# x of tiles 6 to 15 transposed by SBUF-to-SBUF transfers and 32x32 transposes on VectorE, and the low parts of the k and v weights on VectorE

## The chip, the cores and the metric

The kernel runs on one core of one Trainium2 chip. The metric is the device time of one execution in microseconds (us). Before the change its median is 504.29 us over three runs (504.22 to 504.36). Beside these runs one execution was profiled; the rows quoted below are from it, and their times count from the start of its span.

## The reference

x has 2048 positions of 512 features. It is normalised, put through an attention with 32 heads of 16 features, in which each position looks at 8 positions at a distance of 2 (itself, 2 back, ... 14 back), and the result is gated by the silu of a two-layer network on the same normalised x.

```python
def _A_ref(x, wqkv, wo):
    B, S, D = x.shape
    H = 32; Dh = D // H
    W, dil = 8, 2
    qkv = (lambda x, *d: x.transpose(*d))((x @ wqkv).reshape(B, S, 3, H, Dh), 2, 0, 3, 1, 4)
    q, k, v = qkv[0], qkv[1], qkv[2]
    ...
    logits = jnp.einsum("bhsd,bhswd->bhsw", q, kg) * scale
    logits = jnp.where(mask[None, None, :, :], logits, -1e9)
    attn = _softmax(logits, axis=-1)
    o = jnp.einsum("bhsw,bhswd->bhsd", attn, vg)
    return (lambda x, *d: x.transpose(*d))(o, 0, 2, 1, 3).reshape(B, S, D) @ wo

def _B_ref(x, w1, b1, w2, b2):
    h = jnp.einsum("bsd,df->bsf", x, w1) + b1
    zero = jnp.zeros_like(h)
    r = jnp.where(h > zero, h, zero)
    h = r * r
    out = jnp.einsum("bsf,fd->bsd", h, w2) + b2
    return out

x = A_x
xn = _layernorm(x, axis=-1)
s = _A_ref(xn, A_wqkv, A_wo)
g = _silu(_B_ref(xn, B_w1, B_b1, B_w2, B_b2))
return x + s * g
```

## The kernel before

**Numbers in two parts.** Every product is made of three passes (`PASSES`): each operand is split in a high part, which ScalarE copies to the matmul's type (`high`), and a low part, which is the difference (`low`, a subtraction on VectorE or on POOL). High times high, high times low and low times high are added up in PSUM. So a product of a tile with a 512-wide weight is 12 matmuls: four pieces of the inner dimension by three passes.

**Stage 1: tiles of x.** x goes through in 16 tiles of 128 positions, worked in pairs. For a tile `t`, `mean`, `spread` and `norm` compute the normalised rows `xn` on ScalarE and POOL. `trans` turns them with four 128x128 transposes on TensorE into a PSUM tile `pxT` (two buffers), ScalarE copies the high part of the result, and `lowx` makes the low part on VectorE. Then `qkv(t, s)` multiplies by the three parts of wqkv (s = 0, 1, 2 for q, k, v), `evacuate` copies the product to `stg`, and a transfer per pair and part takes it to DRAM (`sq`, `sk`, `sv`). From tile 4 on the transposed tile also goes to DRAM (`sx`), for stage 2.

**Stage 2: the network, in four chunks of four tiles.** For each of 14 slices f of the hidden layer, `up(c, f)` makes the hidden values `ph` (12 matmuls); ScalarE applies relu and squares it twice, once for the high part `h`, once in place; `lowh(f)` makes the low part on VectorE. `down(pb, f, j)` adds its product with w2 to `pb` (12 matmuls for the four tiles). `down` follows `up` two slices behind. `ph` has two PSUM buffers (`psH`), so `up(c, f + 2)` cannot start before `lowh(f)` has read `ph` of slice f. At the end of a chunk `gate` applies the bias `b2t` and silu to `pb`, giving `z`.

**Attention, on VectorE.** It is done in eight units u of 256 positions. q, k, v of a unit are loaded from DRAM. `qk(u, s)` is a multiplication over 128x2048 into `pr` and a reduction of it (a pair), four pairs a unit; `soft_a` and `soft_b` are the softmax around an exponential on ScalarE; `av(u, s)` is a multiplication into `pv` and a reduction into `v`, again four pairs a unit. The stream runs qk of unit u, then av of unit u - 1, the last unit's av at the end. `store(u)` writes the result to DRAM (`so`), `load_o(u)` reads it back in four transfers (`oq`), `trans_o` turns it in 32x32 blocks on VectorE, and `lowo` makes its low part. `out_product` multiplies by wo (`pw`), and `finish` multiplies with `z`, adds x and writes the output.

**The order.** All engines take their instructions in an order that the program fixes. For the attention the program keeps two planned clocks, `clock["PE"]` and `clock["V"]`, which add a price per instruction (227 ns a matmul, 150 ns a transpose, elements over 0.96 plus 170 ns on VectorE). `pump(margin)` puts the next steps of the attention stream into VectorE's queue as long as VectorE's planned clock stays under TensorE's plus the margin. `load_o(u)` needs `store(u)`, and puts whatever is left before it into the queue at once:

```python
    def load_o(u):
        while done_units[0] <= u:
            flush(None)
            pump(clock["V"] - clock["PE"] + 4000)
```

In chunk c, `load_o(2c)` stands at f = 7, ahead of `lowh(7)`, and `load_o(2c + 1)` at f = 12, ahead of `lowh(12)`; `trans_o` of the first two tiles stands at f = 10. For the last chunk, units 6 and 7 are thus stored, read back and transposed within the chunk.

Transfers from SP's queue go in SP's order; loads of q, k, v and of the transposed x (`xU`) go from ScalarE's queue. In the profile all instructions of the helper `Ordered` carry line 76, so rows are told apart by tile names.

Of the kernel before, what the change touches and what calls it, by code (L numbers as in the profile page):

```python
# [8 lines left out]
F32 = mybir.dt.float32  # L9
FR = mybir.dt.float32r  # L10
AF = mybir.ActivationFunctionType
# [25 lines left out]

WARM = 18
WARM2 = 3

MATMUL, TRANSPOSE, DVE_FIXED, SLACK, LATE, ROOM = 227, 150, 170, 500, 3000, 1000

# [4 lines left out]
def body(ctx: ExitStack, tc: tile.TileContext, x, wqkv, wo, w1, b1, w2, b2, out):  # L47
# [119 lines left out]
    mhalf = const.tile([P, 1], F32, name="mhalf")  # L167
    G.memset(mhalf, -0.5)
    mask = const.tile([P, BI, W], F32, name="mask")
    zero = px.tile([HALO, 4, P], F32, name="zero")  # L170

    def constants():
        G.memset(zero, 0.0)
        for t in (sk, sv):
            dma(t[:, :HALO, :].rearrange("g h c -> h g c"), zero)
        G.memset(mask, 0.0)
        for blk in (1, 0):
            for w in range(W):
                n = max(0, min(BI, (W - 1 - w) * DIL - blk * BI))
                if n:  # L180
                    G.memset(mask[:4 * blk + 4, :n, w], -1e9)

    b1t = const.tile([P, NF], F32, name="b1t")
    b2t = const.tile([P, D], F32, name="b2t")

    sq = dram.tile([4, S, P], F32, name="sq")
    sk = dram.tile([4, HALO + S, P], F32, name="sk")
# [187 lines left out]


    NT = S // P
    mv, means, rs, shifts, xn, pTs, xt, xT, seen = {}, {}, {}, {}, {}, {}, {}, {}, {}

    def moments(t, st):  # L380
        mv[t] = px.tile([P, 2], F32, name=f"mv{t}", tag="mv", bufs=2)
# [21 lines left out]
        G.tensor_mul(shifts[t], means.pop(t), rs[t])  # L403

    def norm(t):
        xn[t] = px.tile([P, D], F32, name=f"xn{t}", tag="xn", bufs=2)
        if t < 2:
            n = D // 2 if t == 0 else D
            for i in range(0, D, n):
                V.tensor_scalar(xn[t][:, i:i + n], xins[t][:, i:i + n], mv[t][:, 0:1], rs[t],  # L410
                                op0=OP.subtract, op1=OP.mult)
            del xins[t]
        else:
            A.activation(xn[t], xins.pop(t), AF.Identity, bias=shifts.pop(t), scale=rs[t])
        if t + 4 < NT:
            load_x(t + 4)

    def place(t):
        if t < TPC:
            xt[t] = xT[0][:, t]  # L420
        else:
            xt[t] = pxT.tile([P, 2, KT, P], FR, name=f"xt{t}", tag="xt", bufs=4)

    def trans(t):
        place(t)
        pTs[t] = psT(f"pxT{t}")
        for kt in range(KT):
            PE.transpose(pTs[t][:, kt * P:(kt + 1) * P], xn[t][:, kt * P:(kt + 1) * P], ident)
        seen[t] = clock["PE"] + 800
        A.activation(xt[t][:, 0], pTs[t].rearrange("p (k n) -> p k n", k=KT), AF.Copy)  # L430

    def lowx(t):
# [60 lines left out]

    def lows(s, kt):
        low(*wq_parts(s, kt), V)
        low(*wq_parts(s, kt + 1), G)


    sts = [px.tile([P, 6], F32, name=f"st{t}", tag="st", bufs=2) for t in range(2)]
# [17 lines left out]
    norm(1)  # L517
    for kt in range(1, KT):
        split(*wq_parts(0, kt), V)
    split(xt[0][:, 0], xt[0][:, 1], x0.rearrange("p (k n) -> p k n", k=KT), V)  # L520
    ps = psA("pq0_0")
    for kt in range(KT):
        if kt == KT - 1:
            trans(1)
        PE.matmul(ps, x0[:, kt * P:(kt + 1) * P], raws[0, kt], start=kt == 0, stop=kt == KT - 1)
    lowx(1)
    evacuate(0, 0, ps)
    highs(1, 0)
    lows(1, 0)
# [28 lines left out]
    for a in range(2, NT, 2):  # L558
        b, more = a + 1, a + 2 < NT
        later = a + 4 < NT  # L560

        def weights(f):
            if 0 <= f < NKEEP:
                load_w(keep, f)
            if 0 <= f - 1 < NKEEP:
                split_w(f - 1)

        if later:
            mean(a + 4)
        qkv(a, 0)  # L570
        if more:
            trans(a + 2)
        pump(LATE)
        qkv(b, 0)
        weights(a - 5)
        if more:
            lowx(a + 2)
            trans(b + 2)
        if later:
            mean(b + 4)  # L580
        pump(LATE)
        qkv(a, 1)
        if later:
            spread(a + 4)
        if more:
            lowx(b + 2)
        pump(LATE)
        if not more:
            up(0, 0)
        qkv(b, 1)  # L590
        if later:
            spread(b + 4)
        if not more:
            pump()
            up(0, 1)
            lowh(0)
        weights(b - 5)
        pump(LATE)
        qkv(a, 2)
        if later:  # L600
            norm(a + 4)
        pump(LATE)
        qkv(b, 2)
        if later:
            norm(b + 4)
        if a == NT - 4:
            dma(b1t, b1.rearrange("(f p) -> p f", p=P))
            dma(b2t, b2[None, :].to_broadcast([P, D]))
        if a >= TPC:
            for t in (a, b):  # L610
                dma(sx[t // TPC][:, t % TPC], xt.pop(t).bitcast(F32))
        pump(LATE if more else -SLACK)
# [66 lines left out]
        dma(tile_rows(out, t)[:, cols], z[:, cols])  # L679

    wot = p2.tile([P, 2, 4, 512], FR, name="wot")

    for c in range(NCH):
        last = c == NCH - 1
        pb = [psA(f"pb{c}_{j}") for j in range(TPC)]
        t0 = c * TPC
        for f in range(2, NF):
            if c == 0:
                for i in (6, 7) if f == 2 else (f + 5,):
                    if i < NF:  # L690
                        load_w(p2, i)
            up(c, f)
            pump()
            if c == 0 and f == 3:

                rwo = [p2.tile([P, 2, D], F32, name=f"rwo{i}", tag="oT", bufs=2) for i in range(2)]
                for i in range(2):
                    for q in range(4):
                        rows = wo[q * P + 64 * i:q * P + 64 * i + 64, :].rearrange("(g p) n -> p g n", g=2)
                        dma(rwo[i][32 * q:32 * q + 32], rows)  # L700
            if c == 0:
                if NKEEP <= f + 3 < NF:
                    split_w(f + 3)
                if 6 <= f < 10:
                    split(wot[:, 0, f - 6], wot[:, 1, f - 6], rwo[(f - 6) // 2][:, (f - 6) % 2], G)
            elif f == 2:
                finish(t0 - 4, G)
                finish(t0 - 3, G)
            elif f == 3:
                load_r(t0 - 2)  # L710
                load_r(t0 - 1)
                trans_o(t0 - 2, psT(f"pT{t0 - 2}"))
                trans_o(t0 - 1, psT(f"pT{t0 - 1}"))
            elif f == 4:
                lowo(t0 - 2)
                lowo(t0 - 1)
            elif f == 5:
                out_product(t0 - 2, psT(f"pw{t0 - 2}"))
            elif f == 6:
                finish(t0 - 2, G)  # L720
                out_product(t0 - 1, psT(f"pw{t0 - 1}"))
            elif f == 7:
                finish(t0 - 1, G)
            if f == 7:
                load_o(c * 2)
            if f in (9, 10) and not last:
                load_r(t0 + f - 9)
            if f == 10:
                for i in range(2):
                    trans_o(t0 + i, psT(f"pT{t0 + i}"))  # L730
            if f == 11:
                for i in range(2):
                    lowo(t0 + i)
            if f == 12:
                load_o(c * 2 + 1)
            if not (last and f == NF - 1):
                for j in range(TPC):
                    down(pb, f - 2, j)
            pump(ROOM if c else -SLACK)
            lowh(f)  # L740
        for j in range(2):
            out_product(t0 + j, psT(f"pw{t0 + j}"))
        pump()
        if not last:
            for i in range(2):
                for j in range(TPC):
                    down(pb, NF - 2 + i, j)
                pump()
            for i in range(2):
                up(c + 1, i)  # L750
            for j in range(TPC):
                gate(c, j, pb)
            lowh(0)
            lowh(1)
            pump()
        else:
            for i in range(2, TPC):
                trans_o(t0 + i, psH(f"pT{t0 + i}"))
            for i in range(2, TPC):
                lowo(t0 + i)  # L760
            xl = xTa.tile([P, TPC, 512], F32, name="xlast", tag="xT")
            dma(xl.rearrange("p (h e) n -> p h (e n)", e=2),
                x[t0 * P:(t0 + TPC) * P, :].rearrange("(h p e) n -> p h (e n)", p=P, e=2))
            for j in range(TPC):
                for f in range(NF - 3, NF):
                    down(pb, f, j)
                gate(c, j, pb)
                if j < 2:
                    finish(t0 + j, V, xl[:, j])
            for j in range(2, TPC):  # L770
                n = D // 2 if j == TPC - 1 else D
                for i in range(0, D, n):
                    cols = slice(i, i + n)
                    out_product(t0 + j, (psT if i else psH)(f"pw{t0 + j}_{i}"), cols)
                    finish(t0 + j, V, xl[:, j], cols)


# [19 lines left out]
```

## Time and profile before

| | us |
|---|---|
| median of three runs | 504.29 |
| the profiled execution's own time | 504.34 |
| its span | 502.3 |
| TensorE (PE) busy | 494.2 (98%) |
| VectorE (DVE) busy | 418.1 (83%) |
| ScalarE (ACT) busy | 218.8 (44%) |
| POOL busy | 107.8 (21%) |

The page has an execution in rows by engine. PE is the matmuls, PEld the loading of weights beside them, SPq and ACTq the instructions that issue transfers. A row of the timeline has start and duration in us, engine, line, operation, tile written and tiles read, shapes, how many instructions were merged, and in brackets how long the engine had been idle before and what ended that. In a row of a group the two numbers after the first bar are the busy time in us and the mean duration of one in ns, and after the second bar stands the idle time before. The chain of waits follows the end of the execution back to what released each step.

Stage 1 runs to about 160 us (the products of the last pair are mixed with the first `up`), and the chunks begin at about 141, 231, 318 and 405 us.

### The profile page before, as it was taken

The numbers are of one execution on the slowest core, as the hardware profiler recorded it, in microseconds if no ns is written. First come the engines' busy times: TensorE is split into PE (matmuls) and PEld (weight loads), VectorE is DVE, ScalarE is ACT, GpSimd is POOL, SyncE is SP. The second block draws the span as 40 slices with busy tenths as digits, with TensorE's granted clock in tenths as the row PEclk, the third lists the DMA queues.
The fourth block names the chain that finished last, engine by engine and source line by source line (L and its number), as shares of the span: only waits on it lengthen the run. The fifth ranks groups of instructions, "written<-read, shape, count | busy, mean of one in ns | idle before, by whom it ended". The sixth has DMA issues, their size and how long they took to land.

```text
span 502.3 us, 5930 instructions
## 1 busy us (share of the span) xinstructions
PE 494.2 (98%) x2202; PEld 405.9 (81%) x2202; DVE 418.1 (83%) x334; ACT 218.8 (44%) x397; POOL 107.8 (21%) x125
## 2 busy tenths in 40 slices
PE   8899999999999999999999999999999999999996
PEld 5688888888888888888888888888888888888885
DVE  5217999987999999995799999399899949998926
ACT  5855456663242555513632341362253146414322
POOL 1622345861000588300203000021200002120000
PEclk9999999999999999999999999999999999999999
DMA  8979489689664757261433406125230822311052
GB/s 293 278 245 393 179 260 317 230 277 372 231 240 134 253 146 241 84 242 43 127 157 100 172 11 267 58 85 201 82 148 11 299 67 85 136 64 42 4 164 84
DMA packets 45064, 85.64 MB, mean 171 GB/s; under 512 B 4988, under 2 KB 28908, under 8 KB 42220
## 3 DMA queue, kind: packets, MB, share of 16 engines
q1 hardware_dynamic: 40716, 51.72, 31.2%
q10 hardware_dynamic: 4320, 33.56, 18.1%
q8 instruction: 17, 0.28, 0.2%
q14 instruction: 11, 0.09, 0.1%
HBM read 57.94 MB, written 27.32 MB: 170 GB/s over the span
## 4 chain that ended last, share of the span: by engine, by line
PE 95%; DVE 1%; DMA 1%; POOL 0%; issue 0%; SPq 0%; ACT 0%; DVEq 0%
PE ph L76 30%; PE pb L76 30%; PE pq L76 25%; PE pw L76 8%; PE pxT L76 1%; DMA wqraw<-in_A_wqkv 1%; DVE z L76 1%; DVE wq L76 0%; SPq L144 0%; POOL wq L76 0%; DVE xT L76 0%; SPq L134 0%; POOL rs L76 0%; ACT z L76 0%; ACT stg L76 0%
## 5 line engine op out<-in xcount | busy, mean ns | idle before, releaser
L76 PE MATMUL pb<-w,h 128*128 128x512 f32 x672 | 160.6, 389 | 0.0
L76 PEld LDWEIGHTS pb<-w,h 128*128 128x128 f32 x672 | 126.2, 188 | 26.2
L76 ACT ACTIVATE ph<-ph,b1t 128x512 f32<-128x512 f32 x56 | 37.0, 661 | 196.4 <-PE ph L76 191.9
L76 PE MATMUL ph<-xU,w 128*128 128x512 f32 x504 | 120.7, 390 | 0.0
L76 PEld LDWEIGHTS ph<-xU,w 128*128 128x128 f32 x504 | 94.4, 188 | 20.4 <-DVE h L76 0.9
L76 PE MATMUL pq<-wq,xt 128*128 128x512 f32 x432 | 101.3, 392 | 0.0
L76 PEld LDWEIGHTS pq<-wq,xt 128*128 128x128 f32 x432 | 80.3, 188 | 16.5
L76 DVE TENSOR_TENSOR pr<-k,q 128x2048 f32<-128x2048 f32 x32 | 75.6, 2362 | 10.4 <-DMA k<-sk 10.0
L76 DVE TENSOR_TENSOR pv<-v,L 128x2048 f32<-128x2048 f32 x32 | 75.9, 2373 | 0.4
L76 DVE TENSOR_REDUCE L<-pr 128x128 f32<-128x2048 f32 x32 | 73.1, 2284 | 0.7
L76 DVE TENSOR_REDUCE v<-pv 128x256 f32<-128x2048 f32 x32 | 72.9, 2278 | 0.6
L76 POOL TENSOR_TENSOR z<-z,xr 128x512 f32<-128x512 f32 x12 | 21.2, 1778 | 220.4 <-DVE z L76 215.7
L76 DVE TENSOR_TENSOR h<-ph,h 128x512 fp32r<-128x512 f32 x56 | 38.4, 686 | 31.2 <-ACT ph L76 30.9
L76 ACT ACTIVATE stg<-pq 128x512 f32<-128x512 f32 x48 | 28.6, 596 | 57.8 <-PE pq L76 52.6
L76 PE MATMUL pw<-wot,oT 128*128 128x512 f32 (+1 forms) x204 | 45.5, 376 | 0.0
L76 PEld LDWEIGHTS pw<-wot,oT 128*128 128x128 f32 x204 | 36.8, 188 | 7.1
L76 PE MATMUL ph<-xT,w 128*128 128x512 f32 x168 | 40.5, 390 | 0.0
L76 POOL TENSOR_TENSOR w<-w1r,w 128x512 fp32r<-128x512 f32 x14 | 24.3, 1735 | 68.8 <-ACT w L76 66.2
L76 PEld LDWEIGHTS ph<-xT,w 128*128 128x128 f32 x168 | 31.5, 188 | 6.7
L76 PE MATMUL pq<-wq,xT 128*128 128x512 f32 x132 | 32.9, 402 | 1.8 <-POOL wq L76 1.5
L76 ACT ACTIVATE h<-ph 128x512 fp32r<-128x512 f32 x56 | 33.5, 599 | 1.8
L76 ACT ACTIVATE ph<-ph 128x512 f32<-128x512 f32 x56 | 33.3, 595 | 0.0
(64 smaller groups left out, 318.9 us busy)
## 6 DMA issues: line engine op xcount, KB each, us to landing
k<-sk ACTq DMA_DIRECT2D x8, 1408.0 KB, 8.6
v<-sv ACTq DMA_DIRECT2D x8, 1408.0 KB, 9.4
sx<-xt SPq DMA_DIRECT2D x12, 512.0 KB, 7.6
xU<-sx ACTq DMA_DIRECT2D x6, 1024.0 KB, 8.2
x<-in_A_x SPq DMA_DIRECT2D x16, 256.0 KB, 4.2
sq<-stg SPq DMA_DIRECT2D x8, 512.0 KB, 4.1
sk<-stg SPq DMA_DIRECT2D x8, 512.0 KB, 6.9
sv<-stg SPq DMA_DIRECT2D x8, 512.0 KB, 3.2
```

Source lines behind the costliest of these rows:

```text
L76: return tc.keep_in_program_order(f(*a, **k))
```

## The change

**Tiles 6 to 15 (`TURN` = 6).** `norm` writes a pair of tiles into one buffer, in which the 512 features are grouped in four blocks a, each with the 32 features a of every 128. `shuffle` then moves the pair with four SBUF-to-SBUF transfers of 128 KB each, issued from SP: block a of position 4p + b goes to partition 32a + p, place b. `trans` turns the moved tile `xb` with a single VectorE instruction of 32x32 transposes, whose output in PSUM steps by 4 elements, so that the positions come out in their order. The four TensorE transposes of these tiles are gone; ScalarE's copy and `lowx` stay. `mean`, `spread` and `norm` of the pair after next stand earlier in the loop, and `trans` and `lowx` of the next pair one product later.

**The k and v weights' low parts.** `lows` computes every second one on VectorE in place of POOL, four in all. At the start `lowx(1)` stands ahead of the low part of tile 0.

**Other moves.** `zero` lies in a buffer of the attention's, `b2t` in stage 2's memory and is loaded at its start. The last product of tile 15 is split in 256, 128 and 128 columns, where it was 256 and 256.

```diff
     def lows(s, kt):
         low(*wq_parts(s, kt), V)
-        low(*wq_parts(s, kt + 1), G)
+        low(*wq_parts(s, kt + 1), V)
...
     def norm(t):
-        xn[t] = px.tile([P, D], F32, name=f"xn{t}", tag="xn", bufs=2)
+
+        if t < TURN:
+            xn[t] = px.tile([P, 2, D], F32, name=f"xn{t}", tag="xn", bufs=2)[:, 0]
+        elif t % 2 == 0:
+            xn[t] = px.tile([P, 4, 2, P], F32, name=f"xn{t}", tag="xn", bufs=2)
...
         else:
-            A.activation(xn[t], xins.pop(t), AF.Identity, bias=shifts.pop(t), scale=rs[t])
+
+            A.activation(xn[t // 2 * 2][:, :, t % 2].rearrange("p a (k c) -> p k a c", k=KT),
+                         xins.pop(t).rearrange("p (k a c) -> p k a c", a=4, k=KT),
+                         AF.Identity, bias=shifts.pop(t), scale=rs[t])
...
+    def shuffle(t):
+
+        src = xn.pop(t)
+        xb[t] = px.tile([P, 4, 2, P], F32, name=f"xb{t}", tag="xn", bufs=2)
+        for a in range(4):
+            dma(xb[t][32 * a:32 * a + 32].rearrange("p b e c -> p b (e c)"), src[:, a].rearrange("p e c -> p (e c)"))
+
     def trans(t):
         place(t)
         pTs[t] = psT(f"pxT{t}")
-        for kt in range(KT):
-            PE.transpose(pTs[t][:, kt * P:(kt + 1) * P], xn[t][:, kt * P:(kt + 1) * P], ident)
-        seen[t] = clock["PE"] + 800
+        if t < TURN:
+            for kt in range(KT):
+                PE.transpose(pTs[t][:, kt * P:(kt + 1) * P], xn[t][:, kt * P:(kt + 1) * P], ident)
+            seen[t] = clock["PE"] + 800
+        else:
+
+            V.transpose(out=pTs[t].rearrange("p (k n b) -> p b k n", k=KT, b=4),
+                        in_=xb[t // 2 * 2][:, :, t % 2].rearrange("p b (k c) -> p b k c", k=KT))
+            seen[t] = clock["V"] + 800
         A.activation(xt[t][:, 0], pTs[t].rearrange("p (k n) -> p k n", k=KT), AF.Copy)
...
-    split(xt[0][:, 0], xt[0][:, 1], x0.rearrange("p (k n) -> p k n", k=KT), V)
+    high(xt[0][:, 0], None, x0.rearrange("p (k n) -> p k n", k=KT))
...
     lowx(1)
+    low(xt[0][:, 0], xt[0][:, 1], x0.rearrange("p (k n) -> p k n", k=KT), V)
...
         qkv(a, 0)
-        if more:
+        if a + 2 < TURN:
             trans(a + 2)
+        if later:
+            spread(a + 4)
+            mean(b + 4)
         pump(LATE)
         qkv(b, 0)
         weights(a - 5)
-        if more:
+        if a + 2 < TURN:
+            lowx(a + 2)
+            trans(b + 2)
+        elif more:
+            trans(a + 2)
+        if later:
+            norm(a + 4)
+            spread(b + 4)
+        pump(LATE)
+        qkv(a, 1)
+        if a + 2 < TURN:
+            lowx(b + 2)
+        elif more:
             lowx(a + 2)
             trans(b + 2)
         if later:
-            mean(b + 4)
-        pump(LATE)
-        qkv(a, 1)
-        if later:
-            spread(a + 4)
-        if more:
-            lowx(b + 2)
+            norm(b + 4)
+            shuffle(a + 4)
         pump(LATE)
...
         qkv(b, 1)
-        if later:
-            spread(b + 4)
+        if TURN <= a + 2 < NT:
+            lowx(b + 2)
...
             for j in range(2, TPC):
-                n = D // 2 if j == TPC - 1 else D
-                for i in range(0, D, n):
-                    cols = slice(i, i + n)
-                    out_product(t0 + j, (psT if i else psH)(f"pw{t0 + j}_{i}"), cols)
+                ends = (0, D // 2, 3 * D // 4, D) if j == TPC - 1 else (0, D)
+                for i in range(len(ends) - 1):
+                    cols = slice(ends[i], ends[i + 1])
+                    out_product(t0 + j, (psH, psT, psA)[i](f"pw{t0 + j}_{i}"), cols)
                     finish(t0 + j, V, xl[:, j], cols)
```

More of the change, by code (lines that the diff above doesn't have):

```diff
@@ L39 @@
 WARM2 = 3
+TURN = 6
 MATMUL, TRANSPOSE, DVE_FIXED, SLACK, LATE, ROOM = 227, 150, 170, 500, 3000, 1000
@@ L169, in body @@
     mask = const.tile([P, BI, W], F32, name="mask")
-    zero = px.tile([HALO, 4, P], F32, name="zero")
     def constants():
+        zero = att.tile([P, BI, P], F32, name="zero", tag="q")[:HALO, :4]
         G.memset(zero, 0.0)
@@ L183, in body @@
     b1t = const.tile([P, NF], F32, name="b1t")
-    b2t = const.tile([P, D], F32, name="b2t")
     sq = dram.tile([4, S, P], F32, name="sq")
@@ L377, in body @@
     NT = S // P
-    mv, means, rs, shifts, xn, pTs, xt, xT, seen = {}, {}, {}, {}, {}, {}, {}, {}, {}
+    mv, means, rs, shifts, xn, xb, pTs, xt, xT, seen = ({} for _ in range(10))
     def moments(t, st):
@@ L412, in norm @@
             del xins[t]
-        else:
-            A.activation(xn[t], xins.pop(t), AF.Identity, bias=shifts.pop(t), scale=rs[t])
+        elif t < TURN:
+            A.activation(xn[t], xins.pop(t), AF.Identity, bias=shifts.pop(t), scale=rs[t])
+        else:
+            A.activation(xn[t // 2 * 2][:, :, t % 2].rearrange("p a (k c) -> p k a c", k=KT),
+                         xins.pop(t).rearrange("p (k a c) -> p k a c", a=4, k=KT),
+                         AF.Identity, bias=shifts.pop(t), scale=rs[t])
         if t + 4 < NT:
@@ L599, in body @@
         qkv(a, 2)
-        if later:
-            norm(a + 4)
         pump(LATE)
         qkv(b, 2)
-        if later:
-            norm(b + 4)
         if a == NT - 4:
             dma(b1t, b1.rearrange("(f p) -> p f", p=P))
-            dma(b2t, b2[None, :].to_broadcast([P, D]))
         if a >= TPC:
@@ L681, in body @@
     wot = p2.tile([P, 2, 4, 512], FR, name="wot")
+    b2t = p2.tile([P, D], F32, name="b2t")
+    dma(b2t, b2[None, :].to_broadcast([P, D]))
     for c in range(NCH):
```

## The prediction

> **What bounds the kernel now.** I read the busy shares first, then the chain of waits, then three pieces of the timeline: the first 25 us, VectorE in the last chunk, and the last 25 us.
>
> ```profile
> PE 494.2 (98%) x2202; PEld 405.9 (81%) x2202; DVE 418.1 (83%) x334; ACT 218.8 (44%) x397; POOL 107.8 (21%) x125
> ```
>
> TensorE is busy for 98% of the span, and the chain of waits is TensorE from 19 us to 495 us almost without a gap. So an instruction taken from TensorE is time gained, as long as VectorE, at 83%, still delivers in time. Here is one pair of tiles in stage 1, by the chain (start, us, what):
>
> ```profile
> 66.22 0.44 PE pxT L76 x4
> 66.66 2.75 PE pq L76 x12
> 69.41 0.44 PE pxT L76 x4
> 69.85 13.63 PE pq L76 x60
> 83.48 0.44 PE pxT L76 x4
> ```
>
> A pair takes 83.48 - 66.22 = 17.26 us; five products in a row take 13.63 us, so six take 16.35 us. The two groups of transposes cost 0.91 us a pair.
>
> But VectorE has a deadline of its own in the last chunk. The stretches by busy time (stretch, us, PE, PEld, DVE, ACT, POOL, clock, DMA):
>
> ```profile
> 394.30:478.80 84.50, 84.50 (x373) 69.73 (x372) 73.41 (x58) 30.04 (x50) 7.05 (x4) 1.00 0.28 98
> 478.80:502.30 23.50, 19.19 (x97) 16.18 (x95) 11.35 (x19) 6.72 (x10) 0.00 (x0) 0.95 0.35 113
> ```
>
> VectorE's own rows from there and a little before, and TensorE's last products (start, us, what, idle before it):
>
> ```profile
> 383.40 0.68 DVE L76 TENSOR_TENSOR h<-ph,h 128x512 fp32r<-128x512 f32 x1
> ...
> 418.38 1.31 DVE L76 STREAM_TRANSPOSE pT<-oq 128x512 f32<-128x512 f32 x2
> ...
> 446.20 2.29 DVE L76 TENSOR_REDUCE v<-pv 128x256 f32<-128x2048 f32 x1
> 448.41 0.68 DVE L76 TENSOR_TENSOR h<-ph,h 128x512 fp32r<-128x512 f32 x1
> 449.01 0.68 DVE L76 TENSOR_REDUCE sm_None<-L 128x64 f32<-128x512 f32 x1
> ...
> 451.03 2.29 DVE L76 TENSOR_TENSOR pv<-v,L 128x2048 f32<-128x2048 f32 x1
> ...
> 464.33 0.69 DVE L76 TENSOR_TENSOR h<-ph,h 128x512 fp32r<-128x512 f32 x1 [1.37 <-ACT ph L76]
> ...
> 466.14 2.28 DVE L76 TENSOR_TENSOR pv<-v,L 128x2048 f32<-128x2048 f32 x1
> ...
> 473.57 2.29 DVE L76 TENSOR_REDUCE v<-pv 128x256 f32<-128x2048 f32 x1
> ...
> 487.08 1.32 DVE L76 STREAM_TRANSPOSE pT<-oq 128x512 f32<-128x512 f32 x2 [5.74 <-DMA oq<-so]
> ...
> 488.54 1.29 DVE L76 TENSOR_TENSOR oT<-pT,oT 128x512 fp32r<-128x512 f32 x2
> ...
> 492.24 5.75 PE L76 MATMUL pw<-wot,oT 128*128 128x512 f32 x36
> ...
> 499.12 0.42 DVE L76 TENSOR_TENSOR z<-z,xlast 128x256 f32<-128x256 f32 x1
> ```
>
> The last attention sum ends at 473.57 + 2.29 = 475.86. Its result goes to DRAM and back, and VectorE waits 5.74 us for it. From that transpose at 487.08 to the last addition's end at 499.54 VectorE and ScalarE hand over to each other with no wait for TensorE (12.46 us). So the end is set by the last attention sum as much as by TensorE, and TensorE has little room: the product of tile 14 starts at 492.24 and needs a low part that is ready near 489.2.
>
> **What the change removes.** Ten tiles lose their four TensorE transposes: five pairs of 0.91 us, -4.55 us. In the opening, low parts of wq leave POOL:
>
> ```profile
> 16.81 1.26 POOL L76 TENSOR_TENSOR wq<-wqraw,wq 128x512 fp32r<-128x512 f32 x1
> 16.89 0.81 ACT L76 ACTIVATE xn<-x,shift,rs 128x512 f32<-128x512 f32 x1 [0.47 <-POOL shift L76]
> ...
> 18.13 0.73 PE L76 MATMUL pq<-wq,xT 128*128 128x512 f32 x2 [1.46 <-POOL wq L76]
> ```
>
> and, in the chain,
>
> ```profile
> 18.86 0.44 PE pxT L76 x4
> ```
>
> TensorE stood still 1.46 us for POOL. On VectorE, idle then, that low part is done by 15 us. What is late next is ScalarE's `xn` of tile 2: it ends at 17.70 now, some 0.2 us earlier with the product before it, so the transposes of tile 2 start at about 17.6 and not at 18.86. Tile 3's follow ScalarE's chain in the same way. I take -1.15 us; bounds 0 (ScalarE's chain is held elsewhere) and -1.8 (the whole wait and `lowx(1)`'s place ahead of tile 0's low part).
>
> **What it adds on VectorE.** Ten 32x32 transposes and four low parts in place of POOL's:
>
> ```profile
> L76 DVE STREAM_TRANSPOSE pT<-oq 128x512 f32<-128x512 f32 x16 | 10.5, 701 | 5.7 <-DMA oq<-so 5.7
> ...
> L76 DVE TENSOR_TENSOR wq<-wqraw,wq 128x512 fp32r<-128x512 f32 x8 | 5.4, 698 | 1.8 <-ACT wq L76 1.8
> ```
>
> 14 x 0.70 = 9.8 us. The new transposes write PSUM with a stride, which no row shows; 0.70 is the nearest row, and twice that the upper bound. Each waits for four transfers of 128 KB. Those of `oq` have that size and land in 2.6 to 6.0 us. Stepping through ScalarE's and VectorE's changed queues with these durations, I find 8 to 12 us from `xn`'s end to the transpose, and 6 us or more from a tile's low part to its first product. So I cost the transfers at nothing in stage 1; with that cover gone VectorE waits a few us, and some 3 us that it then has ahead of chunk 0's first `h` take them up. ScalarE's `xn` in blocks (0.81 us each now, at most doubled), `zero` and `b2t` in other memory lie beside busy TensorE: nothing.
>
> **Where the 9.8 us go.** The planner lets VectorE work only so far ahead of TensorE, and TensorE's planned time in stage 1 shrinks too. So the attention stream falls back against TensorE: in the changed program's VectorE queue, two multiply-and-reduce pairs at the start of chunks 1 and 2, two and a half at that of chunk 3, three by its `h_7`. TensorE doesn't mind until something needs attention's result. `load_o(5)` at f=12 of chunk 2 does: it puts three whole pairs ahead of `lowh(12)`. After `h_11`, at 383.40 in both, come 0.6 us and six steps of 2.31 us, so that low part ends near 398.5 in today's times. By the chain
>
> ```profile
> 399.71 5.44 PE pb L76 x24
> ```
>
> TensorE needs it two matmuls into that, at 400.2: just hidden.
>
> In chunk 3 `load_o(6)` at f=7 puts everything left of unit 6 ahead of `lowh(7)`. Between the two transposes of tiles 10, 11 (418.38) and `h_7` (448.41) now stand five pairs; in the changed queue eight, the rest being the same. What a pair costs:
>
> ```profile
> L76 DVE TENSOR_TENSOR pr<-k,q 128x2048 f32<-128x2048 f32 x32 | 75.6, 2362 | 10.4 <-DMA k<-sk 10.0
> ...
> L76 DVE TENSOR_REDUCE v<-pv 128x256 f32<-128x2048 f32 x32 | 72.9, 2278 | 0.6
> ```
>
> A pair is 2.36 + 2.28 = 4.64 us, three are 13.9 us (a step alone is 2.31). The start is 0.2 us earlier, since the turn of the chunk waits for TensorE and ScalarE in both. So `h_7` comes at 448.41 + 13.9 - 0.2 = 462.1 and ends at 462.7, in today's times. It frees the PSUM buffer that `up(3, 9)` needs:
>
> ```profile
> 454.32 2.72 PE ph L76 x12
> ...
> 459.76 2.72 PE ph L76 x12
> ```
>
> **First wait**: TensorE stands from 454.32 to 462.7, 8.4 us. Then `up(9)`, `down(7)`, `up(10)` take 8.16 us and ScalarE 1.85 us (`up(10)` ends at 462.48 now, `h_10` starts at 464.33), so `h_10` starts at 472.7. Behind it in the changed queue stand two `oT` parts, the softmax sums and all four pairs of unit 7; today two of these four are done by then. From `h_10` to the next large step are 1.81 us (464.33 to 466.14), from `sm` to the first `pv` 2.02 us, then four pairs of 4.64 us and `h_11` (0.5 us more): the last sum ends at 472.7 + 1.81 + 2.02 + 18.6 + 0.5 = 495.6, where today it ends at 475.86.
>
> **Second wait**: `h_12` stands behind these pairs, and TensorE waits about 2.3 us for it in `down(12)`; it isn't on the chain that sets the end. **Third wait**: the way of the last unit through DRAM.
>
> ```profile
> 448.52 0.53 SPq L299 DMA_DIRECT2D so<-v x1
> 451.50 2.58 SPq L638 DMA_DIRECT2D oq<-so  x4
> 475.89 0.52 SPq L299 DMA_DIRECT2D so<-v x1
> 478.83 0.40 SPq L762 DMA_DIRECT2D xlast<-in_A_x  x1
> 479.45 1.85 SPq L638 DMA_DIRECT2D oq<-so  x4
> ```
>
> and, over all 32 transfers of `oq`,
>
> ```profile
> DMA to landing us min/median/max: 2.6/3.3/6.0
> ```
>
> Today it takes 487.08 - 475.86 = 11.2 us, with the 1 MB of `xlast` ahead of `oq`. In the changed program `xlast` follows `up(13)` and is in by then: 3.0 us from the store's issue to that of `oq` (448.52 to 451.50), 1.4 to 2.2 us more until the fourth is issued (1.85 and 2.58 less some 0.4 for the last), 3.3 us to land: 7.7 to 8.5 us. The transpose of tiles 14 and 15 comes at 503.3 to 504.1 (506.8 with today's 11.2): 16.2 to 17.0 us after today's, +16.6; at most +19.7. The 12.46 us behind it stay. The last product in quarters adds two small steps on VectorE: +0.1 (TensorE is ahead there).
>
> **TensorE's clock.** An idle TensorE may come back slow. The rows that bear on it:
>
> ```profile
> 1.34 3.94 PE L76 MATMUL warm<-ident 128*128 128x128 f32 x18 [1.34 <-POOL mhalf L76]
> ```
>
> At the start a 128x128 transpose takes 3.94 / 18 = 219 ns, later 0.44 / 4 = 110 ns; and the granted clock of the last 23.5 us is 0.95, which at half rate is 2.35 us, though TensorE is idle for no more than the 4.3 us from 497.99 to 502.3. So about 2 us of idleness seem to be enough. After 8.4 us of waiting the first 3.9 us may run at half rate: 0 to 1.95 us later for `h_10` and all behind it. I take 1.5, nearer to the loss.
>
> The Trainium skill (TensorE: Matmul & The Clock Gate, section "What's actually happening") says that the clock halves after an idle window of some 3.4 us and comes back after as long a busy one. By that rule the wait costs 1.7 us and the sum would be 517.0; with no such gate 515.3.
>
> **Sum**, against the profiled execution's own 504.34 (span 502.3): 504.34 - 4.55 - 1.15 + 16.6 + 0.1 + 1.5 = 516.84. That execution stands 0.05 above the median of the runs: 516.8.
>
> **The rivals.** (1) *Faster*, 498.6 (504.3 - 5.7): VectorE's idle time, 11 us in each late chunk (84.50 - 73.41), takes up the 9.8 us, and no low part is late. For it: today it waits 1.37 and 5.74 us in the rows above. Against: those waits stand at fixed places of the queue, and the eight pairs stand before `h_7`. It decides if `h_7` ends before 454.3. 5%. (2) *Only the first wait counts*: later pairs overlap with TensorE's rest, 504.3 - 5.7 + 8.4 + 1.5 = 508.5. Against it: unit 7's pairs stand behind `h_10`, which TensorE feeds. 8%. (3) *More than that*: the transfers of `xb` and the stores that SP holds behind them are late, or the strided transposes cost twice (7 us more): then the turn of chunk 3 starts late too, with 11.2 us for `oq`, about 522. 9%. The forecast has 78%.
>
> **How the numbers follow.** Within the forecast the bounds give 513.6 (no clock loss, 1.8 us won at the start, 7 us through DRAM: -1.5 - 0.65 - 1.1) to 521.5 (the full 1.95, 11.2 us through DRAM, nothing won at the start: +0.45 + 3.1 + 1.15), and not all of these fall together. I take 512.5 to 521.0, a us lower for a step of the walk that is shorter than counted. That leaves out cases 1 and 2 and part of 3, about 2 in 10. A measurement here can tell 0.2% (1 us) from no change: faster 0.06, same 0.01, slower 0.93.
>
> **What would show it.** Right: the transposes gone from stage 1, TensorE about 5.7 us ahead when chunk 3 starts, then a wait of about 8 us for `h` ahead of one `ph`, a short one in `pb`, and the last transposes of `oq` some 10.8 us later on the clock than 487.08, or 12 with a slow clock. Wrong: TensorE waiting for `xt` in stage 1 (the transfers were not hidden); `h_7` without a wait (the queue is not as late as I count); the last `oq` landing over 9 us after the last sum.

## The result, and the profile after

| | us |
|---|---|
| median before (four runs beside the changed kernel) | 504.33 |
| median after (four runs, 516.22 to 518.02) | 517.03 |
| ratio after to before | 1.0243, 95% interval 1.0224 to 1.0261 |
| the profiled execution's own time, and its span | 518.02, 516.2 |

The changed kernel is 2.4% slower; 516.8 us was predicted. In the page of the changed kernel, the busy times and the engines' shares of the chain of waits (all instructions of the helper carry line 78 now):

```profile
PE 493.7 (96%) x2174; PEld 403.8 (78%) x2174; DVE 425.1 (82%) x350; ACT 218.8 (42%) x397; POOL 91.9 (18%) x121
...
PE 62%; DVE 19%; DMA 6%; issue 5%; ACT 5%; POOL 1%; SPq 0%; ACTq 0%; DVEq 0%; POOLq 0%
```

Forty TensorE transposes are gone, less twelve matmuls that the finer last product adds (2202 to 2174). TensorE is busy only 0.5 us less: the last product takes 1.3 us more (7.08 us against 5.75 us), and the 12 matmuls behind its longest wait 1.7 us more (4.58 us against 2.88 us). The rest isn't accounted for. The span is 13.9 us longer: TensorE's part of the chain falls from 95% to 62%, and VectorE, transfers and their issue fill the rest. What TensorE waited for in the changed kernel (us in total, times, longest):

```profile
PE ph L78 <- DVE h L78: 8.9, 2, 8.4
PE pb L78 <- DVE h L78: 2.5, 1, 2.5
...
PE pq L78 <- DVE xt L78: 0.8, 1, 0.8
```

The large ones are waits for VectorE's low parts. Their places stand in the timeline of the changed kernel, TensorE first:

```profile
447.54 2.88 PE L78 MATMUL pb<-w,h 128*128 128x512 f32 x12
458.82 4.58 PE L78 MATMUL ph<-xU,w 128*128 128x512 f32 x12 [8.40 <-DVE h L78]
...
494.23 7.36 PE L78 MATMUL pb<-w,h 128*128 128x512 f32 x31 [2.48 <-DVE h L78]
```

then VectorE and SP:

```profile
414.36 1.31 DVE L78 STREAM_TRANSPOSE pT<-oq 128x512 f32<-128x512 f32 x2
...
458.09 1.28 DVE L78 TENSOR_TENSOR h<-ph,h 128x512 fp32r<-128x512 f32 x2
...
470.71 0.69 DVE L78 TENSOR_TENSOR h<-ph,h 128x512 fp32r<-128x512 f32 x1 [3.54 <-ACT ph L78]
...
491.29 2.29 DVE L78 TENSOR_REDUCE v<-pv 128x256 f32<-128x2048 f32 x1
...
500.82 1.32 DVE L78 STREAM_TRANSPOSE pT<-oq 128x512 f32<-128x512 f32 x2 [6.05 <-DMA oq<-so]
...
513.25 0.29 DVE L78 TENSOR_TENSOR z<-z,xlast 128x128 f32<-128x128 f32 x1
```

```profile
485.21 0.40 SPq L793 DMA_DIRECT2D xlast<-in_A_x  x1
493.61 0.53 SPq L300 DMA_DIRECT2D so<-v  x1
496.65 1.73 SPq L667 DMA_DIRECT2D oq<-so  x4
```

Read from top to bottom, this is the chain of the prediction. `h_7` (the first of two merged in one row) comes at 458.09, and TensorE stands from 450.42 (447.54 + 2.88) to 458.82. `h_10` follows at 470.71. Behind it VectorE does the whole of the last unit; the last sum ends at 493.58, the store leaves at 493.61, and the last transposes start at 500.82, 13.7 us later than before (487.08). From there to the last addition it is 12.72 us, against 12.46 us.

Three stretches share out the span's 13.9 us. Up to the transposes of tiles 10 and 11 (418.38 before, 414.36 after) the changed kernel is 4.02 us ahead. From there to the last transposes it takes 86.46 us against 68.70 us, 17.76 us more. The tail is 0.26 us longer, and what follows the last addition is 0.1 us shorter.

### The profile page after: what moved, and what is told of

It is laid out like the page before. It is cut to its first block, busy times and chain, and to the rows that moved or that the text cites. A ratio compares the mean times of both kernels' runs of the same rounds, so it can differ in the third digit from the quotient of the medians.

```text
span 516.2 us, 5907 instructions
## 1 busy us (share of the span) xinstructions
PE 493.7 (96%) x2174; PEld 403.8 (78%) x2174; DVE 425.1 (82%) x350; ACT 218.8 (42%) x397; POOL 91.9 (18%) x121
## 4 chain that ended last, share of the span: by engine, by line
PE 62%; DVE 19%; DMA 6%; issue 5%; ACT 5%; POOL 1%; SPq 0%; ACTq 0%; DVEq 0%; POOLq 0%
PE pb L78 24%; PE ph L78 23%; PE pq L78 10%; PE pw L78 5%; DVE pv L78 4%; DVE pr L78 3%; DVE L L78 3%; DVE v L78 3%; DMA xb<-xn 2%; DMA sx<-xt 2%; DVE z L78 1%; DVE h L78 1%; DMA w1r<-in_B_w 1%; ACT scratch L78 1%; DVE oT L78 1%
## 5 line engine op out<-in xcount | busy, mean ns | idle before, releaser
L78 PE MATMUL ph<-xU,w 128*128 128x512 f32 x504 | 122.3, 394 | 8.4 <-DVE h L78 8.4
L78 PEld LDWEIGHTS ph<-xU,w 128*128 128x128 f32 x504 | 95.5, 190 | 29.5 <-DVE h L78 9.7
L78 PE MATMUL pq<-wq,xt 128*128 128x512 f32 x432 | 99.0, 390 | 0.8 <-DVE xt L78 0.8
L78 DVE TENSOR_TENSOR pr<-k,q 128x2048 f32<-128x2048 f32 x32 | 75.7, 2366 | 13.5 <-DMA k<-sk 13.2
L78 DVE TENSOR_TENSOR pv<-v,L 128x2048 f32<-128x2048 f32 x32 | 74.3, 2322 | 0.6
L78 POOL TENSOR_TENSOR z<-z,xr 128x512 f32<-128x512 f32 x12 | 19.3, 1618 | 221.1 <-DVE z L78 163.3
L78 PE MATMUL pw<-wot,oT 128*128 128x512 f32 (+2 forms) x216 | 46.8, 371 | 1.4 <-DVE oT L78 1.4
L78 PEld LDWEIGHTS pw<-wot,oT 128*128 128x128 f32 x216 | 38.0, 188 | 8.9 <-DVE oT L78 1.8
```

The costliest lines, as they stand in the source:

```text
L78: return tc.keep_in_program_order(f(*a, **k))
```

## The experiments

Two names recur: *late* means that pairs of the attention stand ahead of a low part in VectorE's queue, so that it is not there when TensorE needs it; *the way through DRAM* is the time from the end of the last sum to the last transposes of `oq`.

### The same instructions in another order

The planner no longer counts TensorE's transposes of ten tiles, so its TensorE clock runs behind by 4 x 150 ns a tile and it lets fewer attention steps into the queue of stage 1. One line gives that back:

```diff
-            seen[t] = clock["V"] + 800
+            clock["PE"] += 4 * TRANSPOSE
+            seen[t] = clock["V"] + 800
```

> The changed kernel with one line more: the planner goes on counting four TensorE transposes of 150 ns for each tile that now goes through transfers. No instruction is added or taken away; only VectorE's queue is ordered anew (six pairs between the transposes of tiles 10, 11 and h_7 in place of eight; before the change there were five). Theory (the queue fell back against TensorE, h_7 comes late): h_7 ends just ahead of the product that needs it, no wait over 1 us, and the gains of the opening (1.25 us) and of the transposes (4.2 us) stay: 504.3 - 1.25 - 4.2 = 498.9, some 499 to 500.5. Rival A (VectorE simply has 9.8 us more to do, wherever they stand): no better than 515. Rival B (late transfers of xb and what SP holds behind them): about 517, with the same 9.0 us of waiting of pr for k.

Measured: 502.64 us (502.0 to 504.96, 10 runs), ratio 0.9966, interval 0.9951 to 0.9982. VectorE and TensorE have as many instructions as in the changed kernel (350 and 2174). The timeline of this kernel at `h_7` and at the end, TensorE, VectorE and SP in turn:

```profile
448.06 2.88 PE L78 MATMUL pb<-w,h 128*128 128x512 f32 x12
450.80 3.01 PE L78 MATMUL ph<-xU,w 128*128 128x512 f32 x12
```

```profile
450.06 1.28 DVE L78 TENSOR_TENSOR h<-ph,h 128x512 fp32r<-128x512 f32 x2
...
474.99 2.29 DVE L78 TENSOR_REDUCE v<-pv 128x256 f32<-128x2048 f32 x1
...
486.19 1.32 DVE L78 STREAM_TRANSPOSE pT<-oq 128x512 f32<-128x512 f32 x2 [7.72 <-DMA oq<-so]
```

```profile
475.60 0.40 SPq L794 DMA_DIRECT2D xlast<-in_A_x  x1
477.30 0.53 SPq L300 DMA_DIRECT2D so<-v  x1
```

`h_7` starts at 450.06 and TensorE goes on at 450.80: just in time, with two pairs fewer ahead of it. No instruction was taken away, and over 14 us of the loss are gone. So these 14 us hang on the place of VectorE's work, not on its amount, and not on the transfers. The time is still 3.7 us above the 498.9 expected. In this execution the chain of waits ends in the way through DRAM: the last sum ends at 477.28 (475.86 before the change) and the transposes start at 486.19, a way of 8.9 us, with the 1 MB of `xlast` issued 1.7 us ahead of the store; from there the end is fixed. TensorE also waits 1.6 us for `stg` in stage 1, and the first `up` of chunk 0 starts at 137.18, against 135.92 in the changed kernel. What each is worth of the 3.7 us stays open.

### Four steps at each turn of a chunk

`extra(n)` puts n single steps of the attention stream into VectorE's queue whatever the planner says:

```diff
+            extra(1)
             for i in range(2):
                 up(c + 1, i)
             for j in range(TPC):
                 gate(c, j, pb)
+            extra(1)
             lowh(0)
+            extra(1)
             lowh(1)
+            extra(1)
             pump()
```

> The changed kernel, with four single steps of the attention stream forced into VectorE's queue at each turn of a chunk: one ahead of the first two up products, one behind the gates, one behind each of the first two low parts. Work and transfers are those of the change; at the end of chunk 3 all pairs but none are left behind h_10. Theory (the queue fell back): no wait for h_7, h_10 or h_12; the attention is done before today's 475.86; 498.5 to 500.5. A late low part at the turn costs TensorE some us in all four chunks if the four steps (9.2 us) aren't covered there: then up to 503. Rival A (9.8 us more on VectorE, wherever they stand) and rival B (transfers): 515 to 517.

Measured: 501.38 us (500.56 to 501.81, 4 runs), ratio 0.9933, interval 0.9915 to 0.9952. The large waits are gone. Three small ones are left, 2.2 us together: 0.85 us at 155.65, where the changed kernel has 0.47 us, and 1.12 us and 0.21 us at two turns of a chunk. The longest in the timeline of TensorE in this kernel:

```profile
233.24 3.02 PE L78 MATMUL ph<-xU,w 128*128 128x512 f32 x12 [1.12 <-DVE h L78]
```

As a control the same four steps went into the kernel before:

> The kernel before with the same four forced attention steps at each turn of a chunk. Theory: the queue of the kernel before was on time, so the steps win nothing there: 503.5 to 505.5. Rival (earlier attention steps are worth something by themselves, whatever the change): 501 or less.

Measured: 505.97 us (505.89 to 507.79, 10 runs), ratio 1.0031, interval 1.002 to 1.0042, slightly above the expected band. Earlier attention is worth nothing by itself, and the forced steps cost some 1.5 us where nothing was late. With them on both sides, the change wins 505.97 - 501.38 = 4.6 us.

### How many tiles

Each of two kernels moves the point from which tiles go through transfers:

```diff
-TURN = 6
+TURN = 10
...
-            shuffle(a + 4)
+            if a + 4 >= TURN:
+                shuffle(a + 4)
```

> The changed kernel with the transfers for tiles 10 to 15 alone (three pairs in place of five); tiles 6 to 9 are transposed by TensorE again. VectorE's queue has six pairs ahead of h_7. Theory (a threshold: h_7 is either on time or late by pairs): 504.3 - 1.25 - 3 x 0.84 = 500.5, 500 to 501.5, no wait over 1.5 us. Rival (each tile that goes through transfers costs its share): from 503.1 without any to 517.0 with ten, 1.39 us a tile, so six give 511.4.

> The changed kernel with the transfers for tiles 8 to 15 alone (four pairs in place of five). VectorE's queue has eight pairs ahead of h_7, as with five. Theory (threshold): the first wait is there in full, 516.5 to 518, although 1.4 us of VectorE's work and a fifth of the transfers are gone. Rival (each tile costs its share): 503.1 + 8 x 1.39 = 514.2.

The second has `TURN = 8`. Measured: six tiles 503.46 us (503.02 to 503.9, 10 runs), ratio 0.9978, interval 0.9968 to 0.9987; eight tiles 524.51 us (522.64 to 526.94, 4 runs), ratio 1.0396, interval 1.036 to 1.0432. From six tiles to eight it is 21 us, and from eight to ten 7.5 us back: no price per tile does that. The threshold is shown: six pairs stand ahead of `h_7` with six tiles, eight with eight and with ten. Both sizes missed their numbers. With six tiles TensorE waits for no `h`, but the way through DRAM is 9.7 us (the last sum ends at 474.34 + 2.29):

```profile
474.34 2.29 DVE L78 TENSOR_REDUCE v<-pv 128x256 f32<-128x2048 f32 x1
486.32 1.32 DVE L78 STREAM_TRANSPOSE pT<-oq 128x512 f32<-128x512 f32 x2 [8.50 <-DMA oq<-so]
```

With eight, TensorE's timeline has three waits in the place of two:

```profile
399.34 6.86 PE L78 MATMUL pb<-w,h 128*128 128x512 f32 x22 [2.17 <-DVE h L78]
464.51 4.70 PE L78 MATMUL ph<-xU,w 128*128 128x512 f32 x12 [9.14 <-DVE h L78]
501.75 8.93 PE L78 MATMUL pb<-w,h 128*128 128x512 f32 x31 [4.21 <-DVE h L78]
```

The first is `lowh(12)` of chunk 2, the place that the prediction called "just hidden": here four pairs stand ahead of it, and it isn't. In chunk 3 unit 7's four pairs stand behind `h_11` instead of one step ahead of it, so the last unit waits for TensorE once more (1.65 us in VectorE's timeline). I had counted only the pairs ahead of `h_7`, which are eight in both kernels.

### Three pairs left out

```diff
             yield from there("v", u)
+            if u == 3 and s:
+                return
```

> The changed kernel without the last three multiply-and-reduce pairs of the value side of unit 3, three of the four slices of that unit's result stay the unprocessed values. That takes 3 x 4.64 = 13.9 us from VectorE before chunk 3; the transfers, the transposes and the low parts of the change stay. The queue in chunk 3 is on time again. Theory: 504.3 - 1.25 - 4.2 = 498.9, some 498.5 to 500.5, without a wait for h_7. Rival B (transfers of xb and SP's queue): 515 to 517. It doesn't tell the order of the queue from the mere amount of VectorE's work; the kernel with the planner's price and the one with the forced steps do.

Measured: 503.35 us (501.49 to 505.11, 10 runs), ratio 0.9967, interval 0.9949 to 0.9986. Taking 13.9 us of VectorE's work away, far from the place of the wait, removes 13.7 us. By itself that doesn't tell the amount of work from its place; the planner's price does. The time doesn't reach 498.9, and again the chain ends in the way through DRAM: the sum ends at 471.94 + 2.29 = 474.23, the store is issued 0.5 us behind `xlast`, and the transposes come 11.8 us after the sum. VectorE and SP in this kernel:

```profile
471.94 2.29 DVE L78 TENSOR_REDUCE v<-pv 128x256 f32<-128x2048 f32 x1
485.99 1.32 DVE L78 STREAM_TRANSPOSE pT<-oq 128x512 f32<-128x512 f32 x2 [8.69 <-DMA oq<-so]
```

```profile
474.78 0.40 SPq L795 DMA_DIRECT2D xlast<-in_A_x  x1
475.27 0.53 SPq L302 DMA_DIRECT2D so<-v  x1
```

### The parts of the change

No tile through transfers (`TURN = 16` with the condition above), all else as in the change; and every second low part of the k and v weights on POOL again (`V` to `G` in `lows`), with ten tiles:

> The changed kernel with no tile through transfers: TensorE transposes all sixteen. What stays are the low parts of the weights on VectorE, the order of norm, moments and transposes in stage 1, the memory of zero and b2t, and the last product in quarters. Theory (the loss hangs on the ten transposes alone): the gain of the opening, 504.3 - 1.25 = 503.1, 502.6 to 503.6. Rival (the new order in stage 1 or the low parts make the queue late): 508 or more.

> The changed kernel with every second low part of the k and v weights back on POOL. VectorE's queue in chunk 3 has the same order as in the changed kernel. Theory (the loss hangs on the ten transposes; the low parts give the opening's gain): TensorE waits for POOL again in the opening, 517.0 + 0 to 1.25, so 517 to 518.3. Rival (the 2.8 us of low parts on VectorE tip the queue): 500 to 510.

Measured: 503.25 us (502.83 to 505.16, 10 runs), ratio 0.9974, interval 0.9961 to 0.9988; and 518.43 us (518.16 to 519.26, 4 runs), ratio 1.0274, interval 1.0253 to 1.0295. So everything but the tiles is a gain of about 1.2 us, the ten tiles alone bring the loss, and the low parts on VectorE take no part in it (518.43 us is 0.1 us above the expected band). The second kernel's waits show POOL's wait back in the opening:

```profile
PE ph L78 <- DVE h L78: 8.4, 1, 8.4
...
PE pq L78 <- POOL wq L78: 1.5, 1, 1.5
```

### The last way through DRAM

SP's order is told for the last transfers of `oq` and for `xlast`, so that `xlast` comes last; otherwise this is the kernel with the planner's price:

```diff
-            dma(oqs[u][32 * g:32 * g + 32].rearrange("p b e c -> p b (e c)"), src)
+            i = dma(oqs[u][32 * g:32 * g + 32].rearrange("p b e c -> p b (e c)"), src)
+            if u == 2 * NCH - 1:
+                tc.keep_in_program_order(i)
...
-            dma(xl.rearrange("p (h e) n -> p h (e n)", e=2),
-                x[t0 * P:(t0 + TPC) * P, :].rearrange("(h p e) n -> p h (e n)", p=P, e=2))
+            tc.keep_in_program_order(dma(
+                xl.rearrange("p (h e) n -> p h (e n)", e=2),
+                x[t0 * P:(t0 + TPC) * P, :].rearrange("(h p e) n -> p h (e n)", p=P, e=2)))
```

> The kernel with the planner's price, and SP told to issue the 1 MB of xlast behind the last four transfers of oq in place of ahead of the last store. With the price TensorE no longer waited, but the last way through DRAM took 8.92 us (sum to transpose), against 7.24 us in the changed kernel, where xlast was in long before. Theory (that way sets the end by then): 1.7 us less than with the price alone (502.64), 500.9, and TensorE's products become the end. Rival (TensorE's products set the end already, or xlast now comes too late for tile 12): 502.6 or more.

Measured: 502.39 us (500.47 to 503.52, 7 runs), ratio 0.9939, interval 0.9917 to 0.9961. In the profiled execution (500.47 us) the way is 483.07 - 475.80 = 7.27 us, 1.6 us less than with the price alone, as expected:

```profile
473.51 2.29 DVE L78 TENSOR_REDUCE v<-pv 128x256 f32<-128x2048 f32 x1
483.07 1.32 DVE L78 STREAM_TRANSPOSE pT<-oq 128x512 f32<-128x512 f32 x2 [6.07 <-DMA oq<-so]
```

It is the store that lands sooner: 3.0 us after its issue, against 4.5 us with the price alone, 4.4 us with six tiles and 6.5 us with three pairs left out, where `xlast` was issued 0.5 to 1.9 us ahead of it. The chain of waits still ends in this way, not in TensorE's products as expected. Three of the seven runs (500.47 to 500.75 us) lie below all ten with the price alone (502.0 us at the least), the other four don't; what spreads them stays open. So the collision with `xlast` is shown on the way itself, and its worth in the median is not.

### Two steps at each turn

The kernel of four steps showed waits at the turn. Two of the four stand where VectorE idles for ScalarE, and only these are kept; the changed kernel's VectorE there:

```profile
405.86 0.69 DVE L78 TENSOR_TENSOR h<-ph,h 128x512 fp32r<-128x512 f32 x1 [3.79 <-ACT ph L78]
408.58 0.69 DVE L78 TENSOR_TENSOR h<-ph,h 128x512 fp32r<-128x512 f32 x1 [2.02 <-ACT ph L78]
```

```diff
                 gate(c, j, pb)
+            extra(1)
             lowh(0)
+            extra(1)
             lowh(1)
```

It ran with `xlast` issued last (ten tiles, then six), and alone:

> The changed kernel with all ten tiles and two forced attention steps at each turn of a chunk, both where VectorE waits for ScalarE there (behind the gates, and between the first two low parts), and xlast issued behind the last oq. The planner's price is that of the change. Theory (lateness is all that the change loses): no wait of TensorE over 0.5 us in the chunks; the first product of chunk 0 stands 2.9 us earlier than in the kernel without transfers (503.25), so 500.3. Rival (forced steps cost TensorE a wait at the turn, as the four of the earlier kernel did): 501.4 or more.

> Tiles 10 to 15 alone through transfers, with the two forced steps at each turn and xlast behind the last oq. In the kernel with six tiles alone the first product of chunk 0 stood 2.8 us earlier than without transfers, but the last way through DRAM (9.7 us from sum to transpose) set the end. Theory: that is gone, 503.25 - 2.8 = 500.5. Rival (another limit, such as the last additions): 502.5 to 503.5, as before.

> The changed kernel with the two forced attention steps at each turn of a chunk and nothing else: xlast's place on SP is that of the change. Theory (these steps alone take the lateness away, and the attention is then done so early that xlast's place doesn't count): 500.4, as with both edits, 499.8 to 501. Rival (the place of xlast made the gain): 501.5 to 502.6.

Measured, in this order: 500.43 us (500.0 to 501.19, 4 runs), ratio 0.9904, interval 0.9879 to 0.9929; 500.37 us (500.18 to 502.91, 4 runs), ratio 0.9917, interval 0.9886 to 0.9948; 500.39 us (499.66 to 501.55, 6 runs), ratio 0.9918, interval 0.9903 to 0.9934. All three beat the kernel before by their intervals, by 4 us, and the slowest of their runs (502.91 us) is 13 us below the fastest of the changed kernel. That slowest run is the profiled one with six tiles, and there TensorE waits 2.1 us for `h` at the first turn of a chunk. The two steps alone do it, so the place of `xlast` isn't needed. VectorE in the kernel with the two steps alone:

```profile
404.85 0.69 DVE L78 TENSOR_TENSOR h<-ph,h 128x512 fp32r<-128x512 f32 x1 [1.00 <-ACT ph L78]
...
463.81 2.29 DVE L78 TENSOR_REDUCE v<-pv 128x256 f32<-128x2048 f32 x1
476.35 1.31 DVE L78 STREAM_TRANSPOSE pT<-oq 128x512 f32<-128x512 f32 x2
```

A step of 2.28 us fits into a wait of 3.79 us and leaves 1.00 us of it. The last sum ends at 466.10, 27 us earlier than in the changed kernel, and the transposes wait for nothing. TensorE sets the end again; the last pieces of the chain of waits in this kernel:

```profile
479.33 8.16 PE pb L78 x36
487.49 6.80 PE pw L78 x48
```

## Why the prediction was right

The mechanism held step by step, and so did its sizes but for one.

- **The opening**, 1.15 us predicted. The first product that uses `xt` starts at 46.02 before and at 44.76 after (rows below): 1.26 us. The kernel with no tile through transfers confirms it on the clock: 504.44 - 503.25 = 1.2 us.
- **The transposes**, 4.55 us predicted, with the transfers beside them at nothing: the mis-sized term. TensorE's first products of stage 1 for the later tiles, and of chunk 0, in the kernel before,

```profile
46.02 2.24 PE L76 MATMUL pq<-wq,xt 128*128 128x512 f32 x9
140.51 2.94 PE L76 MATMUL ph<-xT,w 128*128 128x512 f32 x12
```

  and in the changed kernel, with the waits on the way:

```profile
44.76 3.59 PE L78 MATMUL pq<-wq,xt 128*128 128x512 f32 x15
111.56 18.63 PE L78 MATMUL pq<-wq,xt 128*128 128x512 f32 x80 [0.84 <-DVE xt L78]
135.92 2.94 PE L78 MATMUL ph<-xT,w 128*128 128x512 f32 x12
155.84 3.01 PE L78 MATMUL ph<-xT,w 128*128 128x512 f32 x12 [0.47 <-DVE h L78]
```

  Between them lie 94.49 us before and 91.16 us after: 3.33 us won, with 0.84 us lost in a wait for `xt`. Then 0.47 us goes in a wait for the second `h` of stage 2, which I had thought free. The 4.55 us themselves hold: the kernel with the two steps alone has the same stage 1, no wait for `xt` there, and 89.80 us between the same two products, 4.7 us won. What failed is the cover. I counted 6 us or more from a tile's low part to its first product; here the low part ends at 111.49, 0.07 us ahead of it. VectorE in the kernel before, then in the changed kernel:

```profile
76.39 2.29 DVE L76 TENSOR_TENSOR pr<-k,q 128x2048 f32<-128x2048 f32 x1 [0.76 <-DMA k<-sk]
```

```profile
87.26 2.29 DVE L78 TENSOR_TENSOR pr<-k,q 128x2048 f32<-128x2048 f32 x1 [9.04 <-DMA k<-sk]
...
110.81 0.68 DVE L78 TENSOR_TENSOR xt<-pxT,xt 128x512 fp32r<-128x512 f32 x1
```

  VectorE waits 9.04 us for `k` (13.2 us in the whole kernel, against 10.0 us before) and then works without a pause up to that low part, which comes late behind it. For `xb` itself VectorE waits 0.9 us in the whole kernel. The load of `k` was issued at 72.30, just ahead of four transfers of `xb` (73.00 to 77.66), and 15.0 us pass until VectorE can use it, against 9.1 us before. That the transfers of `xb` slow this load is likely, and no run separates it. The range that I took for `oq`, 2.6 to 6.0 us, was misread too: it is that of the eight transfers from 400 us on, and over all 32 of the kernel before it is 2.3 to 13.9 us.
- **The first wait**, 8.4 us predicted: 8.40 us. `h_7` was put at 462.1 in the times of before; less the 4.02 us that the stretch starts earlier that is 458.08, and it starts at 458.09.
- **The clock**, 1.5 us taken: `up(9)` took 4.58 us where 12 matmuls take 2.88 us, 1.7 us more.
- **The last sum**, predicted at 495.6 + 1.5 - 4.0 = 493.1 on the changed kernel's clock: 493.58.
- **The second wait**, about 2.3 us: 2.48 us, in `down(12)` as said.
- **The way through DRAM**, 7.7 to 8.5 us: 7.24 us, a little below the range, with `xlast` in long before as said.
- **The sum**: 17.76 us lost between the two transposes, against 16.6 + 1.5 = 18.1 us; 4.02 us won ahead of them, against 5.7 us; the tail 0.26 us, against 0.1 us. The errors add up to 1.5 us (14.0 us lost, against 12.5 us); the profiled execution, 518.02 us, is the slowest of the four, and the median lies 1 us below it. That the median is within 0.3 us of 516.8 is therefore luck. Of the signs named for a wrong forecast one came, TensorE waiting for `xt`, and the last transposes came 13.7 us later than before, not 10.8 or 12: both belong to the mis-sized term.
- **Why the pairs fall back.** The prediction named two causes, 9.8 us of work on VectorE and a planned TensorE time that shrinks. The planner's price alone, with all of the 9.8 us in place, leaves six pairs ahead of `h_7` in place of eight and brings it back just in time. So the work alone doesn't make `h_7` late. Whether the shrunken plan would without the work was not tried.
- **The rivals.** "Faster" (498.6 us) is what the change would be worth where nothing is late; no run reached it, and the two forced steps come within 1.8 us. That VectorE's idle time "takes up the 9.8 us" holds, but only if the queue puts work there. "Only the first wait counts" is out: from `h_10` at 470.71 VectorE works without a pause up to the last sum, as the forecast said. Of "more than that" only the delay in stage 1 came, some 1.7 us of it; the strided transposes cost 716 ns and not twice 700, and the way through DRAM was short.

## What to carry to other kernels

Work moved from the bounding engine to one that is 83% busy was paid here where that engine's queue has a deadline, not where the work was put: list what stands ahead of each instruction that the other engine waits for, and price the list. In a planned order a removed instruction also changes the plan; try the same instructions with the old plan before giving up a change. Look for fixed places where the helping engine idles, and put one step there: here two steps a chunk turned 2.4% slower into 0.8% faster.

## What the runs showed of the hardware

- **The SBUF-to-SBUF transfers took up to 14.4 us.** The landing times of the `xb` transfers (128 KB each) in the changed kernel, all 20:

```profile
DMA to landing us min/median/max: 3.2/7.5/14.4
```

  The 32 transfers of `oq`, of the same size but from DRAM and at other times, took 2.3/4.7/9.1 us in this kernel. The runs don't tell the kind of transfer from the traffic beside it.
- **The strided write to PSUM costs next to nothing**, 716 ns against 700 ns. The new transposes beside those of `oq`, groups of the changed kernel:

```profile
L78 DVE STREAM_TRANSPOSE pT<-oq 128x512 f32<-128x512 f32 x16 | 10.5, 700 | 6.0 <-DMA oq<-so 6.0
L78 DVE STREAM_TRANSPOSE pxT<-xb 128x512 f32<-128x512 f32 x10 | 7.2, 716 | 0.9 <-DMA xb<-xn 0.9
```

- **What a wait costs in clock varies.** In the kernel with the low parts on POOL, TensorE waited as long as in the changed kernel:

```profile
458.20 5.49 PE L78 MATMUL ph<-xU,w 128*128 128x512 f32 x12 [8.41 <-DVE h L78]
...
494.58 8.84 PE L78 MATMUL pb<-w,h 128*128 128x512 f32 x31 [2.47 <-DVE h L78]
```

  After 8.4 us the same 12 matmuls took 5.49 us here and 4.58 us there; after 2.5 us the same 31 took 8.84 us here and 7.36 us there, and the granted clock in the 3.5 us behind that wait is 0.53 here and 1.00 there. With eight tiles it is 0.57 behind the wait of 2.17 us. The Trainium skill (TensorE: Matmul & The Clock Gate, section "What's actually happening") says that the clock halves after an idle window of some 3.4 us and comes back after as long a busy one. An estimate worked out from it is a loss of 1.7 us; the 1.7 us of the changed kernel agrees, the 2.6 us of this one (5.49 less 2.88) is more, and the waits of 2.17 us and 2.47 us that cost clock are shorter than its window.
